# Reordering the first stage of a mixer-MLP kernel: one written-out step list, another load order, another engine for the first roots

## The chip, the cores and the metric

The kernel runs on one core of a Trainium2 chip. TensorE multiplies matrices, VectorE and ScalarE (ACT in the profile) do the work on tiles, GpSimd (POOL) does some small work, and SyncE (SP) issues nearly all transfers. All engines run their own queue of instructions in order and wait for one another through semaphores. The metric is the device time of one execution in microseconds; lower is better. A time is given as the median of several runs.

## The reference

The input x has 2048 rows of 512 values. There are two layers with a residual around each:

```python
h  = gelu(layernorm(x) @ w1)                      # 512 -> 512
c  = 128                                          # four column groups of h
g0 = h[:,  0:128] shifted one row down            # row s reads row s-1
g1 = h[:,128:256] shifted one row up              # row s reads row s+1
g2 = h[:,256:384] shifted two rows down
g3 = h[:,384:512] shifted two rows up             # rows outside the input are zero
x1 = x + concat(g0, g1, g2, g3) @ w2              # 512 -> 512
out = x1 + gelu(layernorm(x1) @ w3) @ w4          # 512 -> 1792 -> 512
```

The layernorm has no weights: subtract the mean, divide by the square root of variance plus 1e-5. All tensors are bf16; sums are kept in fp32.

## The kernel before

**Tiles.** Row s of x belongs to partition s // 16 and tile s % 16, so the 2048 rows make 16 tiles of 128 rows, and a neighbouring row lies in the neighbouring tile at the same partition. Tiles are worked on in pairs: pair p holds tiles 2p and 2p+1. A shift by rows thus turns into reading another tile's columns of `hT`; only at the ends (tiles 0, 1, 14, 15) does a shift cross partitions, and six single columns of zeros in `hT`, the pads, stand for the rows outside the input.

**First layer, per tile q.** `stats(q)` (`st`, line 309) takes the statistics of a row tile on VectorE, `aggr(q)` (`ag`, line 312) makes mean and variance of them. The root 1/sqrt(var + eps) is made in one of two ways. `rstd_act` with `rcp` takes a square root on ACT (line 320) and a reciprocal on VectorE (line 326). `rstd_pool` (`rs`) adds eps on GpSimd (line 333) and raises to the power -0.5 there (line 342). `norm` (line 362) subtracts the mean and multiplies by the root on VectorE. The normalised tile is then transposed into `xT`, either by four TensorE transposes (`peT`, line 384) and an evacuation from PSUM (`evacT`, line 396 on ACT or line 398 on VectorE), or by a transposing DMA issued by SP (`dmaT`, line 372).

**First layer, per pair p.** `mm1` multiplies w1 with the transposed pair, 16 products of 256 columns (line 435). `mm1_by_input` (line 451) does the same for pair 0 in four pieces, by blocks of w1's rows, and into four PSUM banks. `gelu1` (lines 479 to 496) writes the result to `hT`. `mm2(t, b, js)` (line 510) makes tile t of the second product from the four shifted windows j, 512 columns each, into bank b; windows 0 to 3 read tiles t-1, t+1, t-2 and t+2. `add1` (line 522) adds x.

**Second layer.** The tiles are taken in the order 2, 3, ..., 15, 0, 1; position k of that order has the index q = 16 + k in the statistics and in `x1T`. Its roots are made on GpSimd, its first ten norms on ACT (line 357), and all its transposes by SP's `dmaT` into `x1T`. `wide(s)` multiplies w3 with 512 columns of `x1T`, that is with q = 16+4s to 19+4s (line 537), and applies the gelu (line 550). `narrow(s)` multiplies with w4 (line 563), adds x1 (line 577) and stores.

**What sets the order.** The program is a list of calls written out by hand. Each call appends operations to the queues of the engines it uses; a queue runs in the order of the calls. Waits follow from the data: `Prog.order` collects who must come first, and `emit` puts a semaphore wait ahead of an operation for each producer, on its own engine too. So moving a call moves its instructions in the queues of all engines that it uses, and those alone.

**The queues in the head, before.** SP issues x tiles 0 to 3 one by one, w1 in two halves, x tiles 4-5 and 6-7 in pairs, 8-11 and 12-15 in fours, then w2; then `dmaT` of tiles 8 to 15 in order, w3, and the `dmaT` steps of the second layer (w4 in pieces between them). ACT loads its table for the square root at the start and the one for the gelu after the second root of tiles 2-3. GpSimd makes the identity, eps, the -0.5 and the six pads, then the roots from tile 4 on, always for two tiles. TensorE starts with 12 products of ones into a bank that is overwritten later (`keep_warm`, line 595). Tiles 0 to 7 are transposed on TensorE, tiles 8 to 15 by SP. Tile 1's evacuation is VectorE's, the other seven are ACT's.

Of the kernel before, what the change touches and what calls it, by code (L numbers as in the profile page):

```python
# [155 lines left out]


def bass_standalone__mixer_s_mlp__prompt_kernel(
    nc: bass.Bass,
# [25 lines left out]
    with ExitStack() as es:  # L185
# [74 lines left out]
        def consts():  # L260
# [55 lines left out]

        def rstd_act(q):
            g = g_sd[q] = Gen()
            pr.op("act", f"sqrt{q}",
                  lambda e: e.activation(sdv[:, q : q + 2], mv[:, q : q + 2, 1], ACT_F.Sqrt,  # L320
                                         bias=eps_c[:], scale=1.0),
                  r=[g_mv[q], g_mv[q + 1], g_eps], w=[g])

        def rcp(q):
            g = g_sd[q]
            pr.op("dve", f"rcp{q}", lambda e: e.reciprocal(rstd[:, q : q + 2], sdv[:, q : q + 2]),
                  r=[g], w=[g_rstd[q], g_rstd[q + 1]])

        def rstd_pool(q, shift=False):

            g, gm = Gen(), Gen()
            pr.op("pool", f"vpe{q}",
                  lambda e: e.tensor_scalar(vpe[:, q : q + 2], mv[:, q : q + 2, 1], LN_EPS, None,  # L333
                                            ALU.add),
                  r=[g_mv[q], g_mv[q + 1]], w=[g])
            if shift:
                pr.op("pool", f"nm{q}",
                      lambda e: e.tensor_scalar(nmean[:, q : q + 2], mv[:, q : q + 2, 0], -1.0,
                                                None, ALU.mult),
                      r=[g_mv[q], g_mv[q + 1]], w=[gm])  # L340
            pr.op("pool", f"pow{q}",
                  lambda e: e.tensor_tensor(rstd[:, q : q + 2], vpe[:, q : q + 2], neghalf[:],  # L342
                                            ALU.pow),
                  r=[g, g_nh], w=[g_rstd[q], g_rstd[q + 1]])
            if shift:
                pr.op("pool", f"nmr{q}",
                      lambda e: e.tensor_tensor(nmr[:, q : q + 2], nmean[:, q : q + 2],  # L347
                                                rstd[:, q : q + 2], ALU.mult),
                      r=[gm, g_rstd[q], g_rstd[q + 1]], w=[g_nmr[q], g_nmr[q + 1]])

# [236 lines left out]

        def keep_warm(n, b):

            g = bank[b].new()  # L590
            ones = nc.const_aps.tensor(1.0, (P, 512), BF16)

            def f(e):
                for _ in range(n):
                    ins = e.matmul(bankap(b), ones[:, 0:P], ones, start=True, stop=True)  # L595
# [14 lines left out]
        consts()  # L610
        act_table(ACT_F.Sqrt)
        keep_warm(12, 3)


# [27 lines left out]
        def ln2a(k):  # L642
            q = NT + k
            stats(q), stats(q + 1), aggr(q), aggr(q + 1)
            rstd_pool(q, True)

# [28 lines left out]

        st(0), aggr(0), aggr(1)
        rstd_act(0)
        stats(2)
        rcp(0)
        norms(0)  # L680
        tps(0, 4)
        evacT("act", 0)
        stats(3), aggr(2), aggr(3)
        evacT("dve", 1)
        rstd_act(2)
        mm1_by_input(0, 0, (0, 1))
        act_table(ACT_F.Gelu_apprx_tanh, after=[g_sd[2]])
        rcp(2)
        norms(2)
        tps(2, 6)  # L690
        mm1_by_input(0, 0, (2, 3))
        evs(2)
        st(4), scale(4)
        st(6)
        norms(4)
        gelu1(0)
        mm1(1, 4, (0, 1, 2))
        tps(4, 6)
        mm1(1, 4, (3,))
        evs(4)  # L700
        gelu1(1)
        scale(6)
        st(8)
        norms(6)
        mm1(2, 0, (0, 1))
        tps(6, 6)
        mm1(2, 0, (2, 3))
        mm2(2, 4, (0, 1, 2))
        evs(6)
        gelu1(2)  # L710
        scale(8)
        st(10)
        norms(8), viaDMA(8)
        mm1(3, 2)
        gelu1(3)
        scale(10)
        st(12)
        norms(10), viaDMA(10)
        scale(12)
        mm2(2, 4, (3,)), mm2(3, 5)  # L720
        st(14)
        norms(12), viaDMA(12)
        scale(14)
# [75 lines left out]
```

## Time and profile before

| | us |
|---|---|
| median of three runs (138.90 to 139.22) | 139.1 |
| the profiled execution: its own time | 139.52 |
| the profiled execution: span from first to last instruction | 137.7 |
| TensorE busy | 131.2 (95%) |
| VectorE busy | 52.0 (38%) |
| ACT busy | 51.4 (37%) |
| GpSimd busy | 15.8 (11%) |

Lines of the timeline give a start, a duration, the engine, the line of the kernel, the operation, output and input with their sizes, a count when several instructions are merged, and in brackets the idle time before them with what ended it. SPq is SP's issuing of transfers, whose durations are those of the issue and not of the transfer. The chain of work is followed back from the last instruction of the program and is shown in order of time. In a row of a group of instructions stand the count, the busy time, the mean nanoseconds of one, and the idle time before them.

### The profile page before, as it was taken

How to read it: one execution, taken by the hardware profiler on the slowest of the kernel's cores; microseconds unless marked ns; L12 is line 12 of the kernel's file. 1: busy time of each engine (PE TensorE's matmuls, PEld its weight loads, DVE VectorE, ACT ScalarE, POOL GpSimd, SP SyncE). 2: the span in 40 equal slices, each digit the busy share in tenths (PEclk: the TensorE clock that was granted, in tenths of full speed). 3: DMA queues.
4: the chain of work that ended last, by engine and by line, in shares of the span. 5: the costliest groups of instructions: out<-in, count | busy, mean ns of one | idle time of the engine just before them, and what ended most of it. 6: DMA issues, size and time to landing. Idle time of an engine off the chain costs nothing.

```text
span 137.7 us, 1779 instructions
## 1 busy us (share of the span) xinstructions
PE 131.2 (95%) x686; PEld 66.4 (48%) x698; DVE 52.0 (38%) x122; ACT 51.4 (37%) x63; POOL 15.8 (11%) x52
## 2 busy tenths in 40 slices
PE   7677999999999999999999999999999999999993
PEld 3265858665444444444444444444444444444452
DVE  0989999998986620000232000022300002232222
ACT  4196722497555555553000555300055530000000
POOL 2005432553312210000000000000000000000000
DMA  3995054589954699400111100011110001111121
GB/s 110 294 331 179 5 114 89 105 271 309 149 113 86 96 243 260 156 5 0 38 38 38 38 0 5 0 38 38 38 38 0 5 0 38 38 38 38 38 73 41
DMA packets 20119, 12.16 MB, mean 88 GB/s; under 512 B 13712, under 2 KB 19088, under 8 KB 20112
## 3 DMA queue, kind: packets, MB, share of 16 engines
q1 hardware_dynamic: 19968, 12.03, 33.7%
q8 instruction: 5, 0.08, 0.2%
q10 hardware_dynamic: 144, 0.03, 0.1%
q14 instruction: 2, 0.02, 0.0%
HBM read 6.82 MB, written 2.10 MB: 65 GB/s over the span
## 4 chain that ended last, share of the span: by engine, by line
PE 88%; DMA 4%; DVE 2%; SPq 2%; issue 1%; ACT 1%
PE ps L563 35%; PE ps L537 35%; PE ps L510 10%; PE ps L435 8%; DMA x_sb<-in_x_dram 4%; DVE st L309 2%; SPq L239 1%; ACT xT L396 1%; SPq L246 1%; PE ps L384 1%; DVE xn L362 0%; DVE o_sb L577 0%; DVE mv L312 0%
## 5 line engine op out<-in xcount | busy, mean ns | idle before, releaser
L563 PE MATMUL ps<-w_sb,h2T 128*128 128x512 bf16 (+2 forms) x234 | 48.7, 367 | 0.2
L537 PE MATMUL ps<-x1T,w_sb 128*128 128x512 bf16 x219 | 48.6, 379 | 0.3
L550 ACT ACTIVATE h2T<-ps 128x1024 bf16<-128x1024 f32 x28 | 28.6, 1023 | 44.8 <-PE ps L537 44.8
L577 DVE TENSOR_TENSOR o_sb<-ps,x_sb 128x512 bf16<-128x512 f32 (+2 forms) x17 | 11.2, 660 | 75.0 <-PE ps L563 75.0
L563 PEld LDWEIGHTS ps<-w_sb,h2T 128*128 128x128 bf16 x238 | 22.8, 98 | 25.9
L537 PEld LDWEIGHTS ps<-x1T,w_sb 128*128 128x128 bf16 x224 | 21.9, 98 | 26.4
L309 DVE BATCH_NORM_STATS2 st<-x_sb 128x6 f32<-128x512 bf16 x32 | 20.4, 676 | 3.7 <-DMA x_sb<-in_x_dram 3.7
L510 PE MATMUL ps<-w_sb,hT 128*128 128x512 bf16 x61 | 14.3, 380 | 0.2
L435 PE MATMUL ps<-xT,w_sb 128*128 128x256 bf16 x112 | 13.6, 273 | 0.5 <-ACT xT L396 0.4
L435 PEld LDWEIGHTS ps<-xT,w_sb 128*128 128x128 bf16 x112 | 10.7, 98 | 3.1 <-ACT xT L396 1.1
L522 DVE TENSOR_TENSOR x_sb<-ps,x_sb 128x512 bf16<-128x512 f32 x16 | 10.3, 679 | 1.0 <-PE ps L510 0.9
L342 POOL TENSOR_TENSOR rstd<-vpe,neghalf 128x2 f32<-128x2 f32 x14 | 9.9, 707 | 0.7
L362 DVE TENSOR_SCALAR xn<-x_sb,mv,rstd 128x512 bf16<-128x512 bf16 x22 | 8.1, 410 | 3.9 <-POOL rstd L342 3.6
L510 PEld LDWEIGHTS ps<-w_sb,hT 128*128 128x128 bf16 x64 | 6.2, 98 | 6.8 <-ACT hT L496 0.5
L357 ACT ACTIVATE xn<-x_sb,nmr,rstd 128x512 bf16<-128x512 bf16 x10 | 7.5, 809 | 2.6 <-POOL nmr L347 2.6
L496 ACT ACTIVATE hT<-ps 128x1024 bf16<-128x1024 f32 x6 | 6.1, 1022 | 5.8 <-PE ps L435 5.8
L333 POOL TENSOR_SCALAR vpe<-mv 128x2 f32<-128x2 f32 x14 | 3.1, 219 | 30.5 <-DVE mv L312 30.4
L595 PE MATMUL ps<-const-bfloat16-1.0 128*128 128x512 bf16 x12 | 4.3, 532 | 0.8 <-PEq L784 0.8
L396 ACT ACTIVATE xT<-ps 128x512 bf16<-128x512 bf16 x7 | 3.8, 592 | 3.0 <-PE ps L384 3.0
L312 DVE BATCH_NORM_AGGREGATE mv<-st 128x2 f32<-128x6 f32 x32 | 4.5, 170 | 0.0
L384 PE MATMUL ps<-ident,xn 128*128 128x128 bf16 x32 | 2.7, 220 | 1.5 <-DVE xn L362 1.5
L384 PEld LDWEIGHTS ps<-ident,xn 128*128 128x128 bf16 x32 | 2.0, 97 | 2.5 <-DVE xn L362 2.2
(21 smaller groups left out, 15.2 us busy)
## 6 DMA issues: line engine op xcount, KB each, us to landing
w_sb<-in_w_dram SPq DMA_DIRECT2D x4, 512.0 KB, 4.7
out_dram<-o_sb SPq DMA_DIRECT2D x15, 128.0 KB, 1.8
w_sb<-in_w_dram SPq DMA_DIRECT2D x1, 1792.0 KB, 7.9
x_sb<-in_x_dram SPq DMA_DIRECT2D x2, 512.0 KB, 6.6
w_sb<-in_w_dram SPq DMA_DIRECT2D x3, 256.0 KB, 3.9
x_sb<-in_x_dram SPq DMA_DIRECT2D x4, 128.0 KB, 2.5
x_sb<-in_x_dram SPq DMA_DIRECT2D x2, 256.0 KB, 5.2
x1T<-xn SPq DMA_TRANSPOSE x16, 3.8
```

Of the source, the lines that this page charges most:

```text
L309: pr.op("dve", f"st{q}", lambda e: e.bn_stats(st6[:, q, :], a), r=[g], w=[g_st[q]])
L342: lambda e: e.tensor_tensor(rstd[:, q : q + 2], vpe[:, q : q + 2], neghalf[:], ALU.pow),
L357: lambda e: e.activation(xn[:, s, :], a, ACT_F.Identity, bias=nmr[:, q : q + 1], scale=rstd[:, q : q + 1]),
L362: lambda e: e.tensor_scalar(xn[:, s, :], a, mv[:, q, 0:1], rstd[:, q : q + 1], ALU.subtract, ALU.mult),
L435: ins = e.matmul(dst, w1_sb[:, dc, P * fc : P * (fc + 1)], xT[:, dc, 256 * p : 256 * (p + 1)], start=(dc == 0), stop=(dc == DC - 1))
L496: pr.op("act", f"g1_{p}", lambda e: e.activation(o, y, ACT_F.Gelu_apprx_tanh), r=gens, w=[g_h[(j, p)] for j in range(DC)])
L510: ins = e.matmul(bankap(b), hT[:, j, c : c + P], w2_sb[:, j, :], start=(j == 0), stop=(j == DC - 1))
L522: lambda e: e.tensor_tensor(x1_sb[:, t, :], bankap(b), x_sb[:, t, :], ALU.add),
L537: ins = e.matmul(bankap(b + i), w3_sb[:, dc, P * fc : P * (fc + 1)], x1T[:, dc, 512 * s : 512 * (s + 1)], start=(dc == 0), stop=(dc == DC ...
L550: pr.op("act", f"g2_{s}_{fp}", lambda e: e.activation(o, a, ACT_F.Gelu_apprx_tanh), r=gens, w=[g])
L563: ins = e.matmul(ps[:, 512 * b : 512 * b + n], h2T[:, fc, s % 2, P * i : P * (i + 1)], w4_sb[:, fc, c0 : c0 + n], start=(fc == 0), stop=(f ...
L577: lambda e: e.tensor_tensor(o_sb[:, s, 0:n], ps[:, 512 * b : 512 * b + n], x1_sb[:, t, c0 : c0 + n], ALU.add),
```

## The change

The calls from the first `st(0)` up to the load of w3 are replaced by a string, `HEAD`, that is read step by step into the same functions. In it

- the roots of all tiles are made by `rstd_pool` on GpSimd; those of tiles 0 and 1 are made one by one (n = 1), the others for two tiles as before. The square roots on ACT and the reciprocals on VectorE are gone from the program;
- ACT loads the gelu's table at the start, and no other;
- statistics, aggregates and norms come in another order on VectorE (tile 0 is aggregated before tile 1's statistics; tiles 2 and 3 are aggregated before the norms of 1 and 0; some pairs are taken odd tile first);
- tile 1's evacuation goes to ACT, so all eight are there; the order is 1, 0, 3, 2, 4, 5, 7, 6;
- `mm1` of a pair is cut into single groups of 128 output columns (`m1 p b fc`), with transposes and single windows of `mm2` between them;
- `dmaT` is issued in the order 8, 9, 11, 10, 13, 12, 14, 15;
- three more products of ones run on TensorE when tile 1's aggregate is done (`warm 3 3 1`), behind the 12 at the start and ahead of the first transpose.

Besides, x tiles 4-5 are issued ahead of w1's two halves instead of behind them, and the six pads are written by VectorE instead of GpSimd.

```diff
+HEAD = """
+st 0; ag 0; rs 0 1; st 1; ag 1; rs 1 1; st 2; st 3; ag 2; ag 3; warm 3 3 1; rs 2; norm 1; norm 0;
+tp 1 5; tp 0 4; st 4; evA 1; norm 2; norm 3; evA 0; tp 2 6; tp 3 7; st 5; ag 4; ag 5; m1i 0 0 0;
+evA 3; rs 4; m1i 0 0 1; evA 2; m1i 0 0 2; st 6; m1i 0 0 3; norm 4; m1 1 4 3; norm 5; g1 0;
+tp 4 6; st 7; m1 1 4 0; ag 6; ag 7; tp 5 7; rs 6; evA 4; m1 1 4 1; st 9; evA 5; m1 1 4 2; st 8;
+norm 7; m1 2 0 1; ag 8; ag 9; g1 1; m1 2 0 3; rs 8; norm 6; tp 7 7; st 11; m1 2 0 2; evA 7;
+tp 6 6; norm 8; m1 2 0 0; ag 11; evA 6; m2 2 4 0; m2 2 4 1; st 10; m1 3 2 2; norm 9; ag 10; g1 2;
+m1 3 2 0; rs 10; st 13; m1 3 2 1; m1 3 2 3; st 12; m2 2 4 2; dT 8; m2 2 4 3; norm 11; ag 13;
+norm 10; g1 3; m2 3 5 0 1 2 3; st 14; ag 12; dT 9; rs 12; st 15; m2 4 6 0 1 2 3; ag 14; ag 15;
+m1 4 0 3; rs 14; dT 11; m1 4 0 1; norm 13; m1 4 0 0; add 3; norm 14; dT 10; m2 5 7 0 1 2 3;
+add 2; m1 4 0 2; norm 12; norm 15; dT 13; g1 4; dT 12; dT 14; dT 15
+"""
...
-                pr.op("pool", f"pad{j}{i}",
+                pr.op("dve", f"pad{j}{i}",
...
-        def rstd_pool(q, shift=False):
+        def rstd_pool(q, n=2, shift=False):
...
-                  lambda e: e.tensor_scalar(vpe[:, q : q + 2], mv[:, q : q + 2, 1], LN_EPS, None,
+                  lambda e: e.tensor_scalar(vpe[:, q : q + n], mv[:, q : q + n, 1], LN_EPS, None,
...
-                  lambda e: e.tensor_tensor(rstd[:, q : q + 2], vpe[:, q : q + 2], neghalf[:],
+                  lambda e: e.tensor_tensor(rstd[:, q : q + n], vpe[:, q : q + n], neghalf[:, 0:n],
                                             ALU.pow),
...
-        def keep_warm(n, b):
+        def keep_warm(n, b, after=()):
...
-            pr.op("pe", "warm", f, w=[g])
+            pr.op("pe", f"warm{len(after)}", f, r=list(after), w=[g])
...
-        for t in range(4):
-            load_x("sp", t, 1)
+        load_x("sp", 0, 1)
+        load_x("sp", 1, 1)
+        load_x("sp", 2, 1)
+        load_x("sp", 3, 1)
+        load_x("sp", 4, 2)
         load_w("w1", w1_sb, w1, 0, 2)
         load_w("w1", w1_sb, w1, 2, 2)
-        load_x("sp", 4, 2)
         load_x("sp", 6, 2)
...
-        act_table(ACT_F.Sqrt)
+        act_table(ACT_F.Gelu_apprx_tanh)
         keep_warm(12, 3)
...
-        st(0), aggr(0), aggr(1)
-        rstd_act(0)
-        stats(2)
-        rcp(0)
-        norms(0)
...
-        adds(0)
-        mm2s(2, 6)
-        mm1(4, 0)
-        gelu1(4)
-        norms(14), viaDMA(14)
+        steps = {
+            "st": stats, "ag": aggr, "rs": rstd_pool, "norm": lambda q: norm("dve", q), "tp": peT,
+            "evA": lambda q: evacT("act", q), "dT": dmaT,
+            "m1i": lambda p, b, *dcs: mm1_by_input(p, b, dcs),
+            "warm": lambda n, b, q: keep_warm(n, b, [g_mv[q]]),
+            "m1": lambda p, b, *fcs: mm1(p, b, fcs), "g1": gelu1,
+            "m2": lambda t, b, *js: mm2(t, b, js), "add": add1,
+        }
+        for step in HEAD.replace("\n", " ").split(";"):
+            name, *args = step.split()
+            steps[name](*map(int, args))
         load_w("w3", w3_sb, w3)
         adds(2)
```

The two numbers of `rs` are the first tile and the count (two where none is given); those of `tp` are the tile and its bank; `m1 p b fc`, `m1i p b block` and `m2 t b j...` are as above.

More of the change, by code (lines that the diff above doesn't have):

```diff
@@ L334, in rstd_pool @@
                                             ALU.add),
-                  r=[g_mv[q], g_mv[q + 1]], w=[g])
+                  r=g_mv[q : q + n], w=[g])
             if shift:
                 pr.op("pool", f"nm{q}",
-                      lambda e: e.tensor_scalar(nmean[:, q : q + 2], mv[:, q : q + 2, 0], -1.0,
+                      lambda e: e.tensor_scalar(nmean[:, q : q + n], mv[:, q : q + n, 0], -1.0,
                                                 None, ALU.mult),
-                      r=[g_mv[q], g_mv[q + 1]], w=[gm])
+                      r=g_mv[q : q + n], w=[gm])
@@ L341, in rstd_pool @@
             pr.op("pool", f"pow{q}",
-                  lambda e: e.tensor_tensor(rstd[:, q : q + 2], vpe[:, q : q + 2], neghalf[:],
+                  lambda e: e.tensor_tensor(rstd[:, q : q + n], vpe[:, q : q + n], neghalf[:, 0:n],
                                             ALU.pow),
-                  r=[g, g_nh], w=[g_rstd[q], g_rstd[q + 1]])
+                  r=[g, g_nh], w=g_rstd[q : q + n])
             if shift:
                 pr.op("pool", f"nmr{q}",
-                      lambda e: e.tensor_tensor(nmr[:, q : q + 2], nmean[:, q : q + 2],
-                                                rstd[:, q : q + 2], ALU.mult),
-                      r=[gm, g_rstd[q], g_rstd[q + 1]], w=[g_nmr[q], g_nmr[q + 1]])
+                      lambda e: e.tensor_tensor(nmr[:, q : q + n], nmean[:, q : q + n],
+                                                rstd[:, q : q + n], ALU.mult),
+                      r=[gm] + g_rstd[q : q + n], w=g_nmr[q : q + n])
@@ L644, in ln2a @@
             stats(q), stats(q + 1), aggr(q), aggr(q + 1)
-            rstd_pool(q, True)
+            rstd_pool(q, 2, True)
         def ln2b(k):
@@ L674, in last_tile @@
             add2(NT - 1, n, P, "act")
-        st(0), aggr(0), aggr(1)
-        rstd_act(0)
-        stats(2)
-        rcp(0)
-        norms(0)
[L681 to L723, printed above, removed]
-        adds(0)
-        mm2s(2, 6)
-        mm1(4, 0)
-        gelu1(4)
-        norms(14), viaDMA(14)
+        steps = {
[9 more added lines that the diff above has]
+            steps[name](*map(int, args))
         load_w("w3", w3_sb, w3)
```

12 lines of the change are left out of this document (6 added, 6 removed).

## The prediction

> **What bounds the kernel now.** I read the page's head first, then the chain of work in order of time.
>
> ```profile
> span 137.7 us, 1779 instructions
> ...
> PE   7677999999999999999999999999999999999993
> ```
>
> ```profile
> 3.58 5.15 DMA x_sb<-in_x_dram
> ...
> 15.87 0.05 issue
> ...
> 21.28 3.49 PE ps L435 x32
> ...
> 28.25 1.73 PE ps L510 x8
> ...
> 32.21 6.42 PE ps L510 x29
> 38.63 4.32 PE ps L537 x20
> ...
> 135.39 0.29 DVE o_sb L577
> ```
>
> From 15.87 us TensorE runs without a gap to the last add at 135.39. The change touches nothing behind the w3 load, so what it can give is read at one place: the first product of the wide layer (line 537), which begins at 38.63. Behind that stand 99.06 us of dense products, unchanged. The question is when that start moves, and what ends last there: TensorE's own queue, or its inputs. It reads w3 and the transposed tiles x1T 16 to 19 (four dmaT steps, queued on SP behind w3). SP's part of the timeline, and the answer for the fourth of these transposes, issued at 32.09:
>
> ```profile
> 16.10 10.45 SPq L372 DMA_TRANSPOSE xT<-xn  x8
> 26.59 0.58 SPq L246 DMA_DIRECT2D w_sb<-in_w_dram  x1
> ```
>
> ```profile
> L372 SPq DMA_TRANSPOSE x1T<-xn x1: 2382/2382/2382, 32.1 to 32.1; - x1
> ...
> DMA to landing us min/median/max: 6.0/6.0/6.0
> ```
>
> 32.09+6.0 = 38.09 is its landing, so TensorE had only 38.63−38.09 = 0.54 us in hand. A gain on TensorE beyond that runs into this landing. The page's DMA issues give the transits (last column, us from issue to landing) of w3, of the 256 KB weight pieces (two halves of w1 and one of w4), of a pair of x tiles and of a transpose in the head:
>
> ```profile
> w_sb<-in_w_dram SPq DMA_DIRECT2D x1, 1792.0 KB, 7.9
> ...
> w_sb<-in_w_dram SPq DMA_DIRECT2D x3, 256.0 KB, 3.9
> ...
> x_sb<-in_x_dram SPq DMA_DIRECT2D x2, 256.0 KB, 5.2
> ...
> xT<-xn SPq DMA_TRANSPOSE x8, 2.5
> ```
>
> w3 lands at 26.59+7.9 = 34.49, and the fourth transpose's issue (32.09, 2.38 us long instead of 10.45/8 = 1.31) is let go at 34.47, at w3's end. So its time hangs on when w3 is issued.
>
> **The change part by part.** Times of the head, from the full timeline:
>
> ```profile
> 0.76 4.28 PE L595 MATMUL ps<-const-bfloat16-1.0 128*128 128x512 bf16 x12 [0.76 <-PEq L784]
> ...
> 3.41 1.29 DVE L309 BATCH_NORM_STATS2 st<-x_sb 128x6 f32<-128x512 bf16 x2 [3.41 <-DMA x_sb<-in_x_dram]
> ...
> 5.59 0.74 DVE L362 TENSOR_SCALAR xn<-x_sb,mv,rstd 128x512 bf16<-128x512 bf16 x2
> ...
> 6.06 0.72 PE L384 MATMUL ps<-ident,xn 128*128 128x128 bf16 x8 [1.03 <-DVE xn L362]
> ...
> 6.49 0.60 ACT L396 ACTIVATE xT<-ps 128x512 bf16<-128x512 bf16 x1 [1.25 <-PE ps L384]
> ...
> 7.49 1.28 ACT L585 ACT_TABLE_LOAD   x1
> ...
> 8.75 1.28 DVE L309 BATCH_NORM_STATS2 st<-x_sb 128x6 f32<-128x512 bf16 x2 [0.30 <-DMA x_sb<-in_x_dram]
> 8.79 0.20 ACT L585 ACTIVATE warm<-eps_c 128x1 f32<-128x1 f32 x1
> ...
> 8.90 1.07 ACT L396 ACTIVATE xT<-ps 128x512 bf16<-128x512 bf16 x2
> ...
> 9.95 0.60 ACT L485 ACTIVATE hT<-ps 128x512 bf16<-128x512 f32 x1
> 9.95 0.30 DVE L312 BATCH_NORM_AGGREGATE mv<-st 128x2 f32<-128x6 f32 x2
> ...
> 10.34 0.22 POOL L333 TENSOR_SCALAR vpe<-mv 128x2 f32<-128x2 f32 x1 [8.61 <-DVE mv L312]
> 10.44 0.66 ACT L479 ACTIVATE hT<-ps 128x256 bf16<-128x256 f32 x2
> 10.64 0.71 POOL L342 TENSOR_TENSOR rstd<-vpe,neghalf 128x2 f32<-128x2 f32 x1
> 11.46 0.73 DVE L362 TENSOR_SCALAR xn<-x_sb,mv,rstd 128x512 bf16<-128x512 bf16 x2
> ...
> 12.11 0.24 DVE L312 BATCH_NORM_AGGREGATE mv<-st 128x2 f32<-128x6 f32 x2
> ...
> 22.60 1.28 DVE L522 TENSOR_TENSOR x_sb<-ps,x_sb 128x512 bf16<-128x512 f32 x2
> ```
>
> Pitches on VectorE: a stats step 0.60 ((9.95−8.75)/2), a norm 0.33 ((12.11−11.46)/2), an aggregate 0.10; one that reads the stats just before it starts 0.72 after them (the aggregates end at 10.25, each about 0.17 long, so the second began at 10.07). Root on GpSimd: from that start to the norm 11.46−10.07 = 1.39, take 1.37.
>
> *Moved memsets, single table load.* The six column memsets end before VectorE's first data at 3.41: free. GpSimd loses them from a stretch that idles until 10.34. The table load at 7.49 ends at 8.79, its dummy at 8.99, and the evacuations begin at 8.90, so its absence gives ACT 0.1 to 0.2 us there, nothing where the order is new. The Trainium skill, page "ScalarE: Activation LUTs", section "What ACT_TABLE_LOAD costs", states 2.66 us for a switch with its drain; here 8.79−7.49 = 1.30 passes and no drain is seen. By the page the removal could be worth 1.4 us more on ACT; the measurement decides.
>
> *Roots on GpSimd.* Stats and aggregates interleaved: ag0 at 4.12, ag1 at 4.94, st2, st3, ag3 at 6.36, so VectorE is free for norm1 at 6.46. GpSimd: vpe0 at 4.38, power 4.68 to 5.39, vpe1 5.43, power to 6.44. A power on one column isn't in the trace; on two it is 0.71, and the nearest lower row is a plain multiply:
>
> ```profile
> L347 POOL TENSOR_TENSOR nmr<-nmean,rstd 128x2 f32<-128x2 f32 x5 | 1.0, 195 | 0.4
> ```
>
> At 0.71 norm1 starts at 6.55, at 0.20 VectorE's own order ends last, 6.46. I take 6.51, against 5.59 before: 0.92 late. It matters only for TensorE's first tiles, as norm2 hangs on ag3, not on these.
>
> *VectorE, its whole order.* norm0 6.84, st4 7.16 (needs x tiles 4-5), norm2 7.77 (6.36+1.37 = 7.73, or st4's end), norm3 8.10, st5 8.42, ag5 9.14, st6 9.24 (its x tiles keep their place in the queue and landed ahead of 10.17; a short wait is covered by the next one), norm4 9.14+1.37 = 10.51 (11.46 before), norm5, st7, ag7 11.88, norm7 13.25, ag9 13.66, norm8 15.03, norm9 16.04, ag10 16.37, norm11 17.74, norm10 18.15, ag12 19.08, norm13 20.45. GpSimd then holds two roots in a row: the second power can't end before 21.41, norm14 21.52, add2 21.85, norm12 22.46, norm15 22.79, next adds 23.12. Before, these adds began at 22.60: VectorE ends the head 0.52 later, since four waits for a root (0.67 ahead of norm4, 0.36 ahead of norm8, 0.46 ahead of norm13, 0.13 ahead of norm14) outweigh the two reciprocals and the copy it loses.
>
> *TensorE.* All eight evacuations are ACT's now, gelus between them. TensorE's work to the end of mm1 of pair 4 is the same: 32 transposes, 80 products of 256 columns at 3.49/32 = 0.109 and 16 of 512 at 1.73/8 = 0.216, some 14.0 us; before, it ran from 6.06 to 21.28+1.75 = 23.03, so 3.0 idle. After: tp1 0.47 behind norm1 (6.06−5.59) at 6.98, its evacuation 0.43 behind (6.49−6.06) at 7.41, the two done 1.07 later at 8.50; tp2 8.24, tp3 8.57; mm1 of pair 0 from 8.79 to 10.54 (before 7.56, in two halves). From here it is fed: tp4 is reached at 10.98, when norm4's tile is just there. ACT has the gelu of pair 0 (9.95 to 10.44+0.66, 1.15 us) from about 10.72 and behind it the evacuations of tiles 4 and 5, 1.07, to 12.88, so pair 2 starts at 12.94 against 13.51 (0.2 idle). The fill-in halves of mm2 then cover the evacuations and gelus, and mm1 of pair 4 ends at 22.1: 0.95 earlier. Its transposes arrive in time by little: dmaT8 issued at 15.5, dmaT9 1.31 later lands at 19.3, wanted at 19.5; dmaT10 lands at 22.0, wanted at 22.1; dmaT12 22.9+2.5 = 25.4, wanted at 25.5. So the products reach the wide layer at 38.63−0.95 = 37.68.
>
> *SP.* dmaT12 now waits for the late norm12 (22.87), and 14, 15 and w3 queue behind it at 1.31 each: w3 at 22.9+3×1.31 = 26.83, 0.24 later than 26.59. That carries to the fourth transpose: 38.09+0.24 = 38.33. Bounds: if it follows its own normalised tile (VectorE 0.52 late), 38.61; if the last 2 us of its transit belong to one execution only, about 37, where the traffic ahead of it ends (windows below), and TensorE's 37.68 ends last.
>
> *x tiles 4-5 ahead of w1; warm-up.* The tile now stands third behind the four single tiles, issued where w1's first half was:
>
> ```profile
> 2.59 0.43 SPq L246
> ...
> 3.07 0.47 SPq L246
> ```
>
> A half of w1 took 3.9 us, the pair itself 5.15 (the chain), so it lands between 6.5 and 7.74, and is wanted at 7.16. I take 6.6, nearest to the row of the same size at the same place: no cost, and no gain from an earlier landing, since VectorE isn't there before. w1's halves move one place back each, issued at 3.07 and 3.58 and landing at most 5.15 later, 8.2 and 8.7; wanted at 8.79 and 9.66: covered by the transposes, and a delay d of the first half would hold mm1 of pair 0 by d less 0.6. Three gated products take 5.15 to 5.8 of a TensorE that waits till 6.98: nothing, and they break the pause between 5.04 and 6.98.
>
> **Sum.** Start of the wide layer: max(37.68, 38.33+0.05) = 38.38, against 38.63: −0.25. Span 137.45. The profiled execution's own time is 139.52 (1.8 outside the span), 0.4 above the median of 139.1, from which I subtract: 138.85.
>
> **The rivals.**
> 1. *The landing doesn't bind.* These windows (columns: share of TensorE's, weight load's, VectorE's, ACT's, GpSimd's time, clock, DMA share, GB/s) lie ahead of 38.09:
>
> ```profile
> 36.00:37.00 1.00, 1.00 (x7) 0.44 (x5) 1.00 (x3) 0.00 (x0) 0.92 (x3) 1.00 1.30 100
> 37.00:38.00 1.00, 1.00 (x6) 0.45 (x5) 1.00 (x3) 0.77 (x2) 0.13 (x1) 1.00 0.07 8
> ```
>
> DMA share falls to 0.07, about one engine of 16, in the last us: one straggler, perhaps not there next time. Then TensorE's 0.95 counts whole: 138.15. For it: almost all bytes had moved by 37. Against it: the queue holds the same transfers in the same order.
>
> 2. *x tiles 4-5 late, slower.* If the tile keeps its 5.15 us, it lands at 2.59+5.15 = 7.74; st4 at 7.76, norm2 8.36, and the chain behind shifts by 0.59, w3 with it: start 38.97, +0.34, 139.44. It decides from a landing at about 7.4. For it: the only 256 KB x loads took over 5 us. Against: they stood behind 1 MB, here behind 0.5 MB, and w1's half in the same place took 3.9.
>
> 3. *TensorE's clock falls.* Between 5.04 and 8.79 it works only some 1.5 us. If it ran for 4.28 us as the 12 warm-up products did (4.28/12 = 0.357 us for 512 columns against 0.216), it would lose 4.28×(1−0.216/0.357) = 1.7 us: the products reach the wide layer at 39.38, +0.75, 139.85. In the trace a gap of 1.03 (ahead of 6.06) did no such thing. The Trainium skill, "TensorE: Matmul & The Clock Gate", Part 1, says an idle window of about 3.4 us halves the clock; no row here has such a window, and the gated products keep this one shorter.
>
> 4. *The new order does nothing*, as SP's queue and not the head sets the start: the landing follows the tile, 38.61, 139.1.
>
> **How the numbers follow.** About 0.2% (0.28 us) is what a measurement can tell from no change. Chances: my case 0.45, ranging from −0.5 to 0, about two fifths of it beyond −0.28; rival 1 0.32, shrunk by small stalls to −0.3 to −0.95, nearly all faster; rival 2 0.1; rival 3 0.04; rival 4 0.09, half same, half slower. Faster 0.18+0.31 = 0.49; slower 0.1+0.04+0.04, with 0.03 for what I don't see: 0.21; same 0.30. Range 138.0 (rival 1 with a little more) to 139.45 (rival 2). The likeliest case's own range is 138.6 to 139.1.
>
> **What would show it.** Right: norm1 near 6.5, norm4 near 10.5, pair 2 of mm1 near 12.9, w3 issued near 26.8, and a wait of 0.7 us of TensorE ahead of line 537. Wrong: no wait there (rival 1), an idle VectorE ahead of st4 until a DMA (rival 2), products of 256 columns well above 0.109 us apart after 8.8 (rival 3), or mm1 of pair 5 waiting over 0.7 us for dmaT10.

## The result and the profile after

| | before | after |
|---|---|---|
| median of 22 runs each, side by side | 139.82 (138.70 to 141.94) | 138.89 (138.48 to 139.32) |
| median span of those after; of the 70 runs of before beside the first eight experiments | 138.0 to 138.1 | 137.05 |
| the profiled execution: time, span | 139.52, 137.7 | 139.09, 137.3 |
| the first product of the wide layer in it | 38.63 | 38.19 |

The ratio of the two is 0.9941, 95% interval 0.9919 to 0.9962: about 0.8 us faster. Ratios, here and below, leave out runs more than 1.5% above the fastest of their own kernel; where it is these runs that matter, their times are given. Two things stand out beside the gain. The kernel before has a much wider spread than the kernel after, and the three runs that gave its median of 139.1 were three of its lower ones. Part of that spread is TensorE's clock: in 6 of the 70 runs the granted clock was 0.988 over the execution, and these took 141.72 to 142.10.

From the page of the kernel after, its span, TensorE's busy tenths and the transit of w3:

```profile
span 137.3 us, 1790 instructions
...
PE   7879999999999999999999999999999999999993
...
w_sb<-in_w_dram SPq DMA_DIRECT2D x1, 1792.0 KB, 7.3
```

TensorE is full from the fourth of the 40 slices on (before, from the fifth), and w3 took 7.3 us, not 7.9. The chain of waits of the kernel after, from the head to the wide layer (start, duration, what):

```profile
9.66 0.72 POOL rstd L358
...
10.48 0.73 DVE xn L378 x2
...
17.20 2.48 DMA xT<-xn
19.68 0.14 issue
19.82 1.47 PE ps L451 x12
...
38.19 4.32 PE ps L553 x20
```

The chain of before began with the landing of x tiles 4-5 (3.58+5.15). That row is gone. The head's chain is now statistics, roots and norms on VectorE and GpSimd, then one transposing DMA (tile 9), then TensorE. No landing of an x1T tile stands ahead of 38.19. The same places in the timeline:

```profile
4.62 0.58 POOL L358 TENSOR_TENSOR rstd<-vpe,neghalf 128x1 f32<-128x1 f32 x1
...
6.32 0.70 DVE L378 TENSOR_SCALAR xn<-x_sb,mv,rstd 128x512 bf16<-128x512 bf16 x2
...
6.94 0.69 DVE L325 BATCH_NORM_STATS2 st<-x_sb 128x6 f32<-128x512 bf16 x1
...
10.48 0.73 DVE L378 TENSOR_SCALAR xn<-x_sb,mv,rstd 128x512 bf16<-128x512 bf16 x2 [0.64 <-POOL rstd L358]
...
15.52 11.04 SPq L388 DMA_TRANSPOSE xT<-xn  x8
...
19.82 1.47 PE L451 MATMUL ps<-xT,w_sb 128*128 128x256 bf16 x12 [0.25 <-DMA xT<-xn]
...
26.60 0.58 SPq L262 DMA_DIRECT2D w_sb<-in_w_dram  x1
```

Line 6.94 is the statistics of tile 4, with no wait in brackets, where before stood 0.30 for the DMA. Norms 1 and 4 come at 6.32 and 10.48, w3 is issued at 26.60. Ten products of mm2 start at 17.25, one every 0.216 us; the eleventh could have followed at 19.41, so TensorE stood 0.41 us for tile 9 (the 0.25 in the bracket counts from the end of the tenth, which overlaps its successor). The transposing DMA of the fourth x1T tile, asked for by its time of issue:

```profile
L388 SPq DMA_TRANSPOSE x1T<-xn x1: 1636/1636/1636, 32.2 to 32.2; - x1
...
DMA to landing us min/median/max: 5.2/5.2/5.2
```

It landed at 32.24+5.2 = 37.44 (transits are given to a tenth, so such a landing is good to 0.05), some 0.7 ahead of the first product that reads it. In this execution it did not bind.

### The profile page after: what moved, and what is told of

It is laid out like the page before. It is cut to its first block, busy times and chain, and to the rows that moved or that the text cites. A ratio compares the mean times of both kernels' runs of the same rounds, so it can differ in the third digit from the quotient of the medians.

```text
span 137.3 us, 1790 instructions
## 1 busy us (share of the span) xinstructions
PE 131.9 (96%) x689; PEld 66.5 (48%) x701; DVE 51.6 (38%) x125; ACT 50.0 (36%) x60; POOL 18.3 (13%) x52
## 4 chain that ended last, share of the span: by engine, by line
PE 83%; DVE 8%; DMA 4%; POOL 1%; issue 1%; DVEq 0%
PE ps L579 35%; PE ps L553 35%; PE ps L526 8%; PE ps L451 5%; DVE st L325 5%; DVE xn L378 2%; DMA x_sb<-in_x_dram 2%; DMA xT<-xn 2%; POOL rstd L358 1%; DVE mv L328 1%; POOL vpe L349 0%; DVE o_sb L593 0%; DVEq L134 0%
## 5 line engine op out<-in xcount | busy, mean ns | idle before, releaser
L358 POOL TENSOR_TENSOR rstd<-vpe,neghalf 128x2 f32<-128x2 f32 (+1 forms) x17 | 11.8, 695 | 1.0
L349 POOL TENSOR_SCALAR vpe<-mv 128x2 f32<-128x2 f32 (+1 forms) x17 | 3.9, 229 | 27.3 <-DVE mv L328 27.2
L412 ACT ACTIVATE xT<-ps 128x512 bf16<-128x512 bf16 x8 | 4.5, 603 | 5.9 <-PE ps L400 5.9
L611 PE MATMUL ps<-const-bfloat16-1.0 128*128 128x512 bf16 x15 | 5.4, 522 | 0.9 <-PEq L760 0.8
L611 PEld LDWEIGHTS ps<-const-bfloat16-1.0 128*128 128x128 bf16 x15 | 1.8, 127 | 4.0 <-issue 3.2
```

Of the source, the lines that this page charges most:

```text
L358: lambda e: e.tensor_tensor(rstd[:, q : q + n], vpe[:, q : q + n], neghalf[:, 0:n], ALU.pow),
```

## The experiments

| label | kernel | median (range), runs | ratio to before, 95% | wide layer starts |
|---|---|---|---|---|
| e1_before_x_first | before, load order alone | 138.96 (138.89 to 139.61, and one of 494.72), 12 | 0.9955 [0.9925, 0.9984] | 38.00 |
| e2_before_gated | before, gated products alone | 139.79 (139.17 to 142.18), 12 | 1.0009 [0.9981, 1.0037] | 41.28 |
| e3_after_w1_first | after, old load order | 142.03 (139.65 to 142.57), 12 | 1.0048 [1.0005, 1.0092] | 38.69 |
| e4_after_no_gated | after, no gated products | 138.83 (138.37 to 140.16), 12 | 0.9958 [0.9922, 0.9994] | 39.27 |
| e5_after_m2_first | after, mm2 of tile 5 earlier | 138.82 (138.44 to 138.99), 12 | 0.9950 [0.9926, 0.9973] | 37.89 |
| e6_after_roots_act | after, first roots on ACT | 138.74 (138.39 to 139.19), 12 | 0.9938 [0.9907, 0.9968] | 37.75 |
| e7_after_pads_pool | after, pads on GpSimd | 139.13 (138.82 to 139.54), 10 | 0.9966 [0.9941, 0.9991] | 37.80 |
| e8_after_again | after | 138.80 (138.45 to 139.56), 12 | 0.9960 [0.9939, 0.9982] | 38.55 |
| e9_after_w3_split | after, w3 in two parts | 140.78 (140.10 to 141.16), 8 | 1.0092 [1.0059, 1.0126] | 40.01 |
| e10_m2_first_w3_split | e5 and e9 together | 140.98 (140.05 to 141.49), 6 | 1.0117 [1.0074, 1.0161] | 39.00 |
| e11_after_w3_later | after, w3 issued later | 141.31 (140.65 to 142.38), 4 | 1.0145 [1.0087, 1.0203] | 40.03 |
| e12_before_again | before | 140.08, 1 | | 39.16 |

The last column is read from the one profiled execution. The ratio of e3 is that of the five fastest of its twelve runs. One run of e1 took 494.72 us at full clock; nothing on record explains it, and it is not in the ratio. The medians of the kernel before, beside these, were 139.87 (e1 to e4), 139.85 (e5 to e8) and 139.67 (e9 to e12).

### The load order alone, and the kernel before once more

```diff
# e1_before_x_first, from the kernel before
+        load_x("sp", 4, 2)
         load_w("w1", w1_sb, w1, 0, 2)
         load_w("w1", w1_sb, w1, 2, 2)
-        load_x("sp", 4, 2)
```

> The kernel before, with x tiles 4-5 issued ahead of w1 and nothing else. The kernel before scatters from 138.7 to 141.9 us (median 139.8), the changed one from 138.5 to 139.3 (median 138.9); the theories differ in what scatters. Theory A (the landing of x tiles 4-5, on which VectorE waits at 8.75 in the kernel before): the pair lands near 6.2, st4 starts when VectorE is free at 8.44, the scatter falls to below 1 us and the median by 0.3 plus the scatter's half, to about 139.0. Theory B (TensorE's clock, held up by the gated products): scatter and median stay as before, 139.5 to 139.8. Theory C (the order of the steps: TensorE reaches the wide layer 0.45 earlier and the rest is scatter of the last transposes): 139.4 to 139.8 with the same scatter.

> The kernel before once more, for its profile in another execution. Theory A: x tiles 4-5, third from last in a burst behind w1, land later than the 8.73 of the first profile when the time is above 139.5, and VectorE's wait ahead of st4 accounts for the difference one to one.

With nothing but the load order changed, the kernel before runs at 138.96, as fast as the whole change. From the timeline and then the chain of e1:

```profile
2.91 1.45 DVE L309 BATCH_NORM_STATS2 st<-x_sb 128x6 f32<-128x512 bf16 x2 [2.91 <-DMA x_sb<-in_x_dram]
...
8.12 1.28 DVE L309 BATCH_NORM_STATS2 st<-x_sb 128x6 f32<-128x512 bf16 x2
```

```profile
0.76 5.28 PE ps L595 x12
...
7.25 1.28 ACT L585
...
38.00 24.17 PE ps L537 x112
```

The statistics of tiles 4-5 start at 8.12, right behind the norms and with no wait, against 8.75 in the kernel before. The wide layer starts 0.63 earlier, exactly as much. Not all of these 0.63 are the edit's: in that execution x tile 0 was there at 2.91 and not at 3.41, and VectorE was through with its norms at 8.12 and not at 8.75−0.30 = 8.45. The wait of 0.30 is the edit's part.

No load of x stands on the chain of e1. It starts with the twelve warm-up products and goes on over the first transposes and ACT's load of the gelu's table (7.25) to the evacuations behind it. So in the old order, with the pair early, that table load comes to bind; whether its removal would gain something there was not tried.

The kernel before itself, profiled again (e12, timeline and chain):

```profile
9.28 1.29 DVE L309 BATCH_NORM_STATS2 st<-x_sb 128x6 f32<-128x512 bf16 x2 [0.83 <-DMA x_sb<-in_x_dram]
```

```profile
39.16 4.32 PE ps L537 x20
```

Here the same wait is 0.83 instead of 0.30, the statistics start 0.53 later, the wide layer starts 0.53 later (39.16 against 38.63), and the time is 140.08, 0.56 above 139.52. So between these two profiles the wait of VectorE for this one load goes into the time one to one. It differs between executions, which fits the wide spread of the kernel before, and moving the load removes the wait and the spread: ten of e1's eleven other runs lie between 138.89 and 139.20, and all eleven had the full clock.

### The gated products alone, and the old load order

```diff
# e2_before_gated, from the kernel before (keep_warm takes a third argument, as in the change)
         keep_warm(12, 3)
...
+        keep_warm(3, 3, [g_mv[1]])
```

> The kernel before, with the three products gated on tile 1's aggregate and nothing else. Theory A (landing of x tiles 4-5): no change, 139.8 and the wide scatter. Theory B (clock): the scatter shrinks to below 1 us, median about 139.0. Theory C (order): no change. In a profile of a disturbed execution theory B wants products of 256 columns more than 0.109 us apart somewhere ahead of 20 us.

In the kernel before the three products change nothing (1.0009). Its profiled execution was its worst by far, 142.18, and shows what a late load can do. From its chain, its timeline and a table by stretches (the stretch and its length, busy time of TensorE, weight load, VectorE, ACT, GpSimd, then the clock, DMA share and GB/s):

```profile
3.58 6.26 DMA x_sb<-in_x_dram
...
41.28 24.17 PE ps L537 x112
```

```profile
9.86 1.29 DVE L309 BATCH_NORM_STATS2 st<-x_sb 128x6 f32<-128x512 bf16 x2 [1.71 <-DMA x_sb<-in_x_dram]
...
13.05 0.72 PE L384 MATMUL ps<-ident,xn 128*128 128x128 bf16 x8 [1.83 <-DVE xn L362]
...
14.62 1.89 PE L435 MATMUL ps<-xT,w_sb 128*128 128x256 bf16 x8 [0.42 <-ACT xT L396]
```

```profile
14.00:16.00 2.00, 1.58 (x9) 1.01 (x8) 1.96 (x7) 1.48 (x3) 0.83 (x3) 0.60 0.00 0
16.00:18.00 2.00, 2.00 (x16) 1.68 (x15) 1.97 (x7) 1.03 (x2) 0.88 (x2) 0.55 0.03 8
```

The pair took 6.26 us. VectorE stood 1.71 for it, TensorE stood 1.83 for a norm behind it, and after that the granted clock was 0.60 and 0.55: eight products took 1.89 us, twice their 0.87. Late load and fallen clock together cost 2.65 us at the wide layer (41.28 against 38.63).

```diff
# e3_after_w1_first, from the kernel after
-        load_x("sp", 4, 2)
         load_w("w1", w1_sb, w1, 0, 2)
         load_w("w1", w1_sb, w1, 2, 2)
+        load_x("sp", 4, 2)
```

> The changed kernel with w1 issued ahead of x tiles 4-5 again, nothing else. My prediction's rival 2 in the strong form: the pair lands near 8.7 instead of 6.2, st4 waits from 6.95 to 8.75, and as VectorE's chain from norm2 on hangs on it, norm4 comes at about 11.9 instead of 10.48, w3 is issued 1.2 to 1.4 later, and the time is 139.7 to 140.3. Theory A expects the wide scatter as well (over 1.5 us between executions); theories B and C the same shift with the narrow scatter of the changed kernel. If the order alone were what counts and the load hidden, 138.9.

With the old load order the new head is slower than the kernel before. Eight of twelve runs had a granted clock of 0.987 or 0.988 over the execution and took 141.08 to 142.57; the four at 1.0 took 139.65 to 140.74. The profiled one is the best of these (timeline, then chain):

```profile
7.98 0.69 DVE L325 BATCH_NORM_STATS2 st<-x_sb 128x6 f32<-128x512 bf16 x1 [1.36 <-DMA x_sb<-in_x_dram]
...
9.04 0.72 PE L400 MATMUL ps<-ident,xn 128*128 128x128 bf16 x8 [1.59 <-DVE xn L378]
```

```profile
38.69 24.21 PE ps L553 x112
```

The new order wants tile 4 at about 6.6 and gets it at 7.95, though the pair took only 4.38 us this time; TensorE stands 1.59. So the two halves of the change are not independent: the new order asks for the pair earlier and has nothing else to do in the pause. Without the load order it pays for the wait, and in most runs with the clock as well.

### The new order without the gated products

```diff
# e4_after_no_gated, from the kernel after
-st 0; ag 0; rs 0 1; st 1; ag 1; rs 1 1; st 2; st 3; ag 2; ag 3; warm 3 3 1; rs 2; norm 1; norm 0;
+st 0; ag 0; rs 0 1; st 1; ag 1; rs 1 1; st 2; st 3; ag 2; ag 3; rs 2; norm 1; norm 0;
```

> The changed kernel without the three gated products, 12 at the start as before. Theory A and C: no change, 138.9 with a narrow scatter, since TensorE waits for tile 1's norm there anyhow. Theory B: the scatter comes back, median 139.5 to 140, and a disturbed profile shows slow products after the pause from 5.3 to 6.8.

The median does not move (138.83). But two of twelve runs, 139.87 and 140.16, show the clock at 0.988. One is the profiled one. Its timeline and its stretches behind the pause, and then the same stretches of the kernel after:

```profile
6.76 0.72 PE L400 MATMUL ps<-ident,xn 128*128 128x128 bf16 x8 [1.33 <-DVE xn L378]
```

```profile
8.00:10.00 2.00, 1.82 (x13) 1.58 (x14) 1.84 (x6) 1.03 (x3) 0.57 (x2) 0.52 0.90 294
10.00:12.00 2.00, 2.00 (x14) 1.49 (x13) 1.52 (x6) 0.33 (x1) 0.38 (x1) 0.63 1.00 375
```

```profile
8.00:10.00 2.00, 1.82 (x20) 1.60 (x21) 1.84 (x6) 1.34 (x3) 0.57 (x2) 1.00 0.92 290
10.00:12.00 2.00, 2.00 (x24) 1.72 (x23) 1.52 (x6) 1.34 (x5) 0.37 (x1) 1.00 0.97 368
```

TensorE is as busy in both, with 27 instructions done against 44. The clock fell after a pause of 1.33 us, which the gated products cut to 0.48. The length of a pause does not decide alone, though: one of 2.13 us in e11 (below) cost no clock. The two stretches of e4 that end and begin with the fall:

```profile
4.66:8.07 3.41, 1.48 (x12) 0.59 (x10) 3.29 (x11) 0.88 (x2) 2.35 (x5) 1.00 0.90 267
8.07:11.48 3.41, 3.30 (x20) 2.62 (x21) 2.77 (x9) 1.29 (x3) 0.94 (x2) 0.50 0.95 334
```

The clock was halved for 3.41 us, as in e2 (14.39 to 17.80), and in the 3.41 us ahead of it TensorE had worked 1.48 us (1.39 in e2). The traces record the clock from its rise on (4.66 in e4). Counted from there in steps of 3.41 us, the eight other profiles with such a record have no step with less than 1.67 us of work (e3), and none of them shows a fall; the first step of the kernel after has 2.42. A limit between 1.48 and 1.67 us of work in such a step would fit all ten, which is an inference from two falls. It would also fit that only some runs of a kernel are hit, since the rise lies anywhere between 3.70 (e6) and 6.02 (e3).

The kernel after (22 runs, and 12 more in e8) and the variants e5, e6 and e7 (34 runs) showed no run with a lower clock. Of the 18 runs of e9 to e11, which keep the products and the load order too, one did (142.38 in e11, not the profiled one). Two in 12 against one in 86 is evidence, not proof. The products cost nothing that these medians show, and with the pair in time they seem to insure against a loss of about 1.2 us. Against the pause that a late pair makes behind them they do not: e2 and e3 have them.

The Trainium skill, "TensorE: Matmul & The Clock Gate", Part 1, names an idle window of about 3.4 us ahead of the fall. The length agrees with the 3.41 us above, the idleness does not: TensorE worked 1.48 us of it in e4 and 1.39 in e2, and the pauses were 1.33 and 1.83. Taken as a pause of 3.4 us, that rule would have excluded rival 3 here.

### What remains of the new order

```diff
# e5_after_m2_first, from the kernel after
-... m2 4 6 0 1 2 3; ag 14; ag 15;
+... m2 4 6 0 1 2 3; m2 5 7 0 1 2 3; ag 14; ag 15;
-m1 4 0 3; ... dT 10; m2 5 7 0 1 2 3;
+m1 4 0 3; ... dT 10;
```

> The changed kernel with one step moved: the second product of tile 5 (m2 5 7) ahead of mm1 of pair 4 instead of in its middle. In the changed kernel's profile TensorE stands 0.41 us (19.41 to 19.82) until the transpose of tile 9 lands, issued 0.4 later than I had it because that of tile 8 took 1.64 us to issue. Theory: that wait is what the new order loses against my sum; the moved step (0.86 us) covers it, the next wait is for tile 10's transpose (landing 22.3, reached at 22.0), so the wide layer starts 0.2 to 0.25 earlier, 138.65 against 138.9, and below the order of before with x tiles first (138.96). Rival: the landing of the fourth x1T transpose (37.44 in the changed kernel) ends last and eats it: 138.9.

This gives TensorE eight more products ahead of tile 9, and the wait for it is gone (chain):

```profile
17.48 3.02 PE ps L526 x14
20.50 3.53 PE ps L451 x32
...
37.89 4.32 PE ps L553 x20
```

The wide layer starts at 37.89 against 38.19, and yet the median, 138.82, is that of the unchanged kernel (138.80 in e8). The other profiles make the size plain. Taken in the same way (2.16 us after the ten products begin), TensorE's wait for tile 9 is 0.41 in the kernel after, 0.29 in e6, 0.11 in e11, 0.07 in e9, and nothing in e7; in e4 and e8 TensorE was late itself. That is some 0.18 us in the mean, estimated from five executions, and these medians don't resolve it. (The 37.73 in the expectation of e10 below is from the timeline, where the kernel after has 38.03; the difference is 0.30 in either view, not 0.46.)

```diff
# e6_after_roots_act, from the kernel after
-        act_table(ACT_F.Gelu_apprx_tanh)
+        act_table(ACT_F.Sqrt)
...
-st 0; ag 0; rs 0 1; st 1; ag 1; rs 1 1; st 2; st 3; ag 2; ag 3; warm 3 3 1; rs 2; norm 1; norm 0;
+st 0; ag 0; st 1; ag 1; sq 0 2; tb; st 2; st 3; ag 2; ag 3; warm 3 3 1; rs 2; rc 0 2; norm 1; norm 0;
```

Here `sq` is the square root on ACT, `rc` the reciprocal, and `tb` the second table load.

> The changed kernel with the root of tiles 0 and 1 made as before, by a square root on ACT and a reciprocal on VectorE, and with the two table loads that this needs; all else as changed. Theory (the part is worth nothing, since VectorE comes to norm1 only after the aggregates of tiles 2 and 3 and norm2 hangs on the root of those): norm1 at 6.45 to 6.5 instead of 6.32, the rest as in the changed kernel, 138.9 to 139.0. Rival (the roots on GpSimd or the single table load are worth their 1.3 us of ACT): above 139.3, with evacuations of tiles 1 and 0 held up behind the second table load.

With two table loads and the first roots back on ACT the kernel runs at 138.74, no slower; taking them away earned nothing in this order. (The roots of tiles 2 and 3, which ACT made too in the kernel before, stay on GpSimd in e6.) ACT's timeline in e6 says why:

```profile
4.96 1.28 ACT L601 ACT_TABLE_LOAD   x1
...
6.99 1.08 ACT L412 ACTIVATE xT<-ps 128x512 bf16<-128x512 bf16 x2 [0.53 <-PE ps L400]
```

The second load ends ahead of the first evacuation, and ACT has nothing else to do there. The Trainium skill, "ScalarE: Activation LUTs", section "What ACT_TABLE_LOAD costs", has a price of 2.66 us for a switch; the load here takes 1.28, as the row shows. By the page's figure it would have lasted until 4.96+2.66 = 7.62, an estimate, and held the evacuation that began at 6.99; the trace does not agree.

```diff
# e7_after_pads_pool, from the kernel after
-                pr.op("dve", f"pad{j}{i}",
+                pr.op("pool", f"pad{j}{i}",
```

> The changed kernel with the six pad columns written by GpSimd as before. Both sides end before the first data: no difference, 138.9. If VectorE's part were worth anything, GpSimd's first root would start later than 4.31 in the profile.

> The changed kernel as it is, beside the others on the same chip: 138.9, scatter below 1 us.

The median of e7 is 0.33 above that of e8, but the median spans are 136.85 and 137.0. The difference lies outside the span: 2.25 to 2.36 us in all ten runs of e7, 1.77 to 1.89 in every run of the kernels before and after and of e1 to e6 and e8. In the program itself the pads' place makes no difference. What the extra half microsecond is, these runs do not show; the kernel before has its pads on GpSimd too, and has 1.8.

The two profiles show the range of the changed kernel. The chain of e7 at the wide layer, and its fourth x1T transpose:

```profile
37.68 0.11 issue
37.80 4.48 PE ps L553 x20
```

```profile
L388 SPq DMA_TRANSPOSE x1T<-xn x1: 1946/1946/1946, 32.1 to 32.1; - x1
...
DMA to landing us min/median/max: 5.5/5.5/5.5
```

With no wait for tile 9 TensorE was through at 37.68. The tile landed at 32.12+5.5 = 37.62, and with the 0.14 us from a landing to the first product (19.68 to 19.82 in the chain after) that holds it until 37.76. Here the landing did bind, by 0.11. In e8 x tiles 6-7 were late instead (timeline, chain):

```profile
10.61 0.69 DVE L325 BATCH_NORM_STATS2 st<-x_sb 128x6 f32<-128x512 bf16 x1 [1.47 <-DMA x_sb<-in_x_dram]
```

```profile
4.05 6.54 DMA x_sb<-in_x_dram
...
38.55 4.40 PE ps L553 x20
```

They took 6.54 us from 4.05, VectorE stood 1.47 in the middle of the head, and the wide layer started at 38.55. The pair behind w1 is now tiles 6-7 (4.5 us in the kernel after, 5.6 in e7, 6.5 here), and part of the scatter that is left comes from there. Another part is x tile 0, which landed at 2.88 in e6 and at 3.36 in e5.

### Does the landing hang on w3's issue?

```diff
# e9_after_w3_split, from the kernel after (e10: the same on e5)
-add 2; m1 4 0 2; norm 12; norm 15; dT 13; g1 4; dT 12; dT 14; dT 15
+add 2; m1 4 0 2; norm 12; norm 15; dT 13; g1 4; dT 12; dT 14; w3 0 1; dT 15; w3 1 3
...
-        load_w("w3", w3_sb, w3)
```

> The changed kernel with w3 loaded in two parts, one block of rows ahead of the transpose of tile 15 and the other three behind it, instead of whole behind it. In all traces so far the fourth x1T transpose lands 10.6 to 11.5 us after w3's issue, and in one (pads on GpSimd) TensorE waited 0.28 us for it ahead of the wide layer. Theory (that landing is the floor under the fastest executions, 138.4 to 138.5, and TensorE's own arrival the median): the landing comes about 1 us earlier, near 36.3; the median of 138.8 stays within 0.1, the fastest may go below 138.4. Rival (the landing binds in most executions): median 138.4 or less. Other rival (the transpose of tile 15 now lands behind a part of w3, later than 29.2): slower, 139 or more.

> Both: the second product of tile 5 ahead of mm1 of pair 4, and w3 in two parts. The moved product alone gave 138.82 against 138.80, though its profile starts the wide layer at 37.73, 0.46 earlier than the changed kernel's. Theory (each alone is stopped by the other limit: TensorE's arrival or the landing): together 138.5, scatter below 0.6 us. Rival (the head's loads, tiles 0 and 6-7, set the time whatever follows): 138.8 as before.

```diff
# e11_after_w3_later, from the kernel after: w3 behind the first x1T transpose
-            viaDMA(q)
+            dmaT(q)
+            if k == 0:
+                load_w("w3", w3_sb, w3)
+            dmaT(q + 1)
...
-        load_w("w3", w3_sb, w3)
```

> The changed kernel with w3 issued one place later, behind the first x1T transpose (28.12) instead of ahead of it, so about 2.9 us later. Theory of my prediction (the landing of the fourth transpose hangs on w3's issue, 10.6 to 11.5 us behind it, with some 0.2 to 0.75 us in hand): landing at about 29.5+9 to 11 = 38.5 to 40.5, wide layer 0.5 to 2.5 us later than 38.0, time 139.4 to 141.3, and TensorE idle ahead of line 553. If the hand were larger, 138.9.

Splitting w3 to land it earlier made the kernel about 1.3 us slower than the kernel before. The timeline of e9, and the transfers issued in the stretch 24 to 35 us (KB each, us to landing):

```profile
29.83 1.91 PE L451 MATMUL ps<-xT,w_sb 128*128 128x256 bf16 x16 [0.58 <-DMA xT<-xn]
...
40.01 1.67 PE L553 MATMUL ps<-x1T,w_sb 128*128 128x512 bf16 x7 [1.36 <-DMA x1T<-xn]
```

```profile
w_sb<-in_w_dram SPq DMA_DIRECT2D x1, 1344.0 KB, 9.0
w_sb<-in_w_dram SPq DMA_DIRECT2D x1, 448.0 KB, 3.7
```

Tile 15's transpose, now behind the first part, came late (3.69 us instead of 2.5), and the larger part took 9.0 us for 1344 KB where the whole took 7.3 for 1792 KB. w3 ended at 27.26+9.0 = 36.26 and the fourth x1T tile landed at 39.87. My expectation fell, and its second rival, a late tile 15, is what happened; e10, with the same split, failed the same way. In e11, with w3 issued at 29.39, the last landing moved with it (timeline):

```profile
29.39 0.58 SPq L262 DMA_DIRECT2D w_sb<-in_w_dram  x1
...
40.03 1.67 PE L553 MATMUL ps<-x1T,w_sb 128*128 128x512 bf16 x7 [2.13 <-DMA x1T<-xn]
```

The tile landed at 39.89, 10.5 us behind w3's issue. With w3 whole, this distance is 11.5 in the kernel before (26.59 to 38.09), 10.84 after (26.60 to 37.44), 11.17 in e7 (26.45 to 37.62), and 10.58 in e5 (26.69 to 37.27). So the landing does hang on w3, at a distance that varies by about 1 us, and in the changed kernel it ends at or just ahead of TensorE's own arrival.

Counted from w3's landing instead of its issue the distance is steadier: 3.6 us before (34.49 to 38.09), 3.5 after, 3.6 in e9 (36.26 to 39.87) and 3.1 in e11, and between 3.1 and 3.6 in all fourteen profiles but one (1.9 in e2, which issues these transposes late). The varying transit of w3 is most of the scatter, and the split failed because it made w3 land later.

## Why the prediction was right, and where it was not

The time (138.85 against 138.89), the range and the sign came true. The argument did so in part only: two errors cancelled. The gain was forecast at 0.25 us and measured at about 0.8, and the base from which it was subtracted was 0.7 too low. That 138.85 met 138.89 is luck.

**Right: the head, step by step.** Norm 4 was put at 10.51 and came at 10.48; norm 1 at 6.51, came at 6.32, since x tile 0's statistics began 0.10 earlier (3.31) and the power on one column took 0.58 (between the bounds 0.20 and 0.71) and ended at 6.07, so that VectorE's own order came last; w3's issue at 26.83, came at 26.60; the pair at 6.6, landed at 2.59+3.6 = 6.19 (e1's took 3.8). Pair 2 of mm1 was put at 12.94, and its first weights are loaded at 12.86. TensorE's arrival at the wide layer, 37.68, is the figure that e7's chain shows. The steps costed at nothing were worth nothing in the medians: table load and first roots (e6), gated products (e2, e4), pads by the span (e7).

**Wrong: the base.** I subtracted the gain from 139.1. The profiled execution (139.52) stood 0.4 above it, and the later runs have the median at 139.8. The wait of 0.30 us for x tiles 4-5, quoted in the prediction's own fence, was the sign: a wait for a transfer at that place is a draw from a spread, and three runs do not show its middle.

**Wrong: "no cost, and no gain" for x tiles 4-5.** This term is the gain. For the changed order it holds that VectorE is not there earlier; but the 0.95 by which I had the new order arrive earlier contained the wait that the load order takes away. The load order alone has the whole effect as far as the medians tell (e1 0.9955 beside 0.9941), and the new order alone has a loss (e3). In the kernel before the price is 0.30 (profile), 0.83 (e12) or 1.71 (e2) us, one to one in the time as far as e12 shows. The bound beside it, w1 landing at most 5.15 behind its issue, did not always hold either: in e8 the second half took 6.4, and TensorE waited 0.34 for it.

**Mis-sized: the landing at 38.33, and so the start at 38.38.** The mechanism stands (e11). But the transit was built from one execution, 11.5 us from w3's issue to the landing, and others have 10.5 to 11.3 (9.4 in e2). With w3 taking 7.3 instead of 7.9 the tile landed at 37.44. With the 0.14 from a landing to the first product (the sum had 0.05) the bound lay at about 37.6, beside TensorE's 37.68, not 0.65 behind it, and rival 1 (the landing doesn't bind; −0.95 us) was nearer to what happened than my own case (−0.25). The wait of 0.7 us ahead of the wide layer, which was to show the step right, is not there in the kernel after, and 0.11 in e7. Set against 139.82 its −0.95 gives 138.87; but it was counted from a profile with a wait of 0.30, so that this meets the median is in part luck too.

**Mis-sized in the profiled execution: tile 9 "lands 19.3, wanted 19.5".** dT8's issue took 1.64, dT9 began at 17.20, landed at 19.68, and TensorE stood 0.41. The twelve products behind that wait took 1.47 us, where e7, without it, has 1.31. So the start gained 0.44 there (38.63 to 38.19) and not 0.95. That the profile's gain (0.43 in time) lies near my 0.25 is thus a coincidence; in other profiles of this order the wait is 0 to 0.29.

**The other rivals.** Rival 2 (the pair late) and rival 3 (the clock) did not occur in the kernel after, but both are real: e3 has both, e4 the second, e2 both in the old order. I had them as separate; a late pair can make the pause behind which the clock falls, and in e4 the plain wait for norm 1 did. Rival 4 (nothing) is excluded by the interval.

**What stays open.** The order of the head as such: e1 (138.96) and the kernel after (138.89, 138.80) cannot be told apart by their medians, so I can't say that it gives anything beyond the load order. There is a hint that it does: no run of e1 was below 138.89, and 19 of the 34 runs of the kernel after (with e8) were, down to 138.45. No kernel tried clearly beats the changed one; e5 and e6 lie within 0.1 us of it. Not explained are the longer transfer of a split w3 and the 0.5 us outside the span in e7.

## What to carry to other kernels

A short wait for a DMA in one profile is one draw: look at the spread of the runs and at a second profile before pricing it, because the median may hold twice as much. When several edits come together, cost the load order against the old instruction order as well as the new one; here one line of it carried the gain as far as the medians tell, and the rewritten order only became harmless with it. Make transits from more than one execution when two arrivals lie within a microsecond of each other, since then the larger of the two is decided by their scatter.

## What the runs showed of the hardware

- A pair of x tiles (256 KB) issued right behind the four single ones landed in 3.6 to 4.5 us (after, e1, e4 to e11). Behind w1's 512 KB it took 4.4 to 6.3 (tiles 4-5 in before, e2, e3, e12), and behind w1 and that first pair 4.5 to 6.5 (tiles 6-7 in after, e1, e4 to e11).
- The granted clock fell to 0.50 for 3.41 us (e2, e4) behind 3.41 us in which TensorE had worked 1.39 and 1.48; with 1.67 or more (e3 and seven others) no fall was seen. Three products of 512 columns raised the 1.48 of e4 to 2.42 in the kernel after.
- A copy of 1792 KB ahead of transposing DMAs took 7.2 (e5) to 7.9 us (before); cut in two around one of them, its larger part of 1344 KB took 9.0 (e9) and 8.4 (e10), and that transpose 3.7 and 3.6 instead of 2.5. The fourth transpose behind it landed 3.1 to 3.6 us after it, 1.9 in e2.
- The issue of a transposing DMA in the head took 1.64, 1.69 and 1.52 us in three executions (tile 8 after, tile 9 in e4, tile 8 in e6) and 1.19 to 1.34 otherwise.
